# An attention and maxout kernel whose written order and list of masked tiles are replaced

## The chip, the core and the metric

The kernel runs on one core of one Trainium2 chip. The core has five engines that run side by side and wait for each other by semaphores: TensorE (PE in the profile, with PEld for its weight loads), VectorE (DVE), ScalarE (ACT), GpSimd (POOL) and SyncE (SP), which here only issues DMAs. The metric is the device time of one execution in microseconds (us), as the median of several runs.

## The reference, cut to what matters

The first part is attention over 8 batches of 8 heads, 576 tokens and 64 columns a head, in which only scores near a row's maximum count; the second is a feed-forward layer whose hidden value is the largest of three products.

```python
scores = scale * np.matmul(q, k.transpose(0, 1, 3, 2))
thresh = np.max(scores, axis=-1, keepdims=True) - tau
scores = np.where(scores >= thresh, scores, -1000000000.0)
scores = scores - np.max(scores, axis=-1, keepdims=True)
attn = np.exp(scores)
attn = attn / (np.sum(attn, axis=-1, keepdims=True) + 1e-09)
attn_out = np.matmul(attn, v)
...
x = attn_out.transpose(0, 2, 1, 3).reshape(B * S, H * D)
h = np.maximum(np.maximum(x @ w1, x @ w2), x @ w3)
out = h @ w_out
```

tau is 0.02, x is 4608 x 512, the hidden layer has 768 columns. Inputs and output are float32.

## The kernel before, in words

**Tiling.** Four heads of a batch make a quad; there are 16 quads. A quad has 9 chunks of 128 score rows in each of two halves r, so there are 144 chunks and 288 score tiles of 128 x 576. A tile's PSUM space is one of four slots of two banks; all of PE's results share these four slots. A score tile is made of two (for a quad's ninth-token chunk, index 4, four) matmuls on the two halves of PE's rows, in float32.

**One score tile.** After PE has made the scores (S), DVE takes their row maximum (m). There are two ways from there, and the string MASKED says for each tile which one is taken. In the *unmasked* way (0) DVE only reads the scores for the maximum ("unused" in the profile); ACT reads them from PSUM, subtracts the threshold and flattens what lies above (e, z<-sc,nm), and a second ACT pass over z makes the exponentials and their sum (n, z<-z). In the *masked* way (1) DVE's maximum pass also writes the negated scores to z in SBUF, so PSUM is free after it; ACT makes exponentials of z (e, z<-z,nm), and a second DVE pass compares with the threshold, multiplies and sums (k, SCALAR_TENSOR_TENSOR z<-z). Then DVE takes the reciprocals of both halves' sums (r), POOL scales both z to bfloat16 P (two p), and SP issues a transposing DMA of P (t). z has four buffers for each half r, so a chunk's z are free for the fourth chunk after it once POOL has read them. P has six buffers.

**The rest.** q and k are transposed on PE (T) and copied out by ACT (a, q) and DVE (c, k); POOL makes a copy of q with halves swapped (q) and casts v (y) and the FFN's weights (z). Once a quad's chunks are transposed, PE multiplies them by v (O), and ACT or DVE copies the result to xt (x, w). Then comes the FFN of a batch: 18 hidden pieces (6 column groups times 3 weights, tile ph) whose results ACT copies (h) and DVE joins by maximum (v), two output pieces (tile po), copied by ACT (u) and stored by SP (o), and a piece for the ninth chunk ("ninth", obr). Hidden and output pieces come in two halves on PE, F and B; B waits for the end of F, as both add to the same PSUM. The last batch's FFN is split in two parts, and its pieces aren't halved. l and g are the loads of q, k, v and of weights, issued by SP.

**What sets the order.** The string ORDER is read letter by letter at the end of the kernel, and `issue` sends each piece of work to its engine; a digit behind S, T, O or F is the PSUM slot. A small wrapper chains the instructions of each engine in that sequence, so each engine executes its own part of the text strictly in order:

```python
        def run(*a, **kw):
            ins = fn(*a, **kw)
            if self._last is not None:
                self._tc.add_manual_dep(
```

All instructions go through it, and so all have the line of its call, L91, in the profile: tiles tell them apart. Which tile comes next is fixed by the loops; only the interleaving of the kinds of work, the slot of each piece and the way of each tile (`masked`, line 311) are in the two strings. A prologue of its own (`beginning`) transposes the first quad and makes the first two score tiles.

Of the kernel before, what the change touches and what calls it, by code (L numbers as in the profile page):

```python
# [39 lines left out]
ORDER = """  # L40
lllllmlyelgS2ymylS3emgnlT0mleS1lakS2nlqermS3ylmeS0pmeS1kpS3elmS2nlzmelrmnT1pS0tcnperkT1pameS1zmteS3knpS0rnmp
emS2permeqS1mnqT3meqktepS0ncS2ntrpmS3npretprmeS1pmnS0tpmS3npmS1etpmeS0rT2mnplkeT1akgeS2qmgepmteS3rkpekntS0pe
rrnmT2pncS3ptamepS1meqtrS2meyqnS3lmqeS0pmelpknT1lpS2nmeymeS3lrkepS0tcnT2rpnmS1tpnmaprrmS0eS2pmteS1pmT3epctep
meT3O0ykntnyS2etrykpnO1wnprmaS0xptrS3meS2zmeS1mzgeS0mlnS3pmleS1pmelO2qmelpkteO0nrnklpS3nlwgxprrmS2leS0pmeF3q
tmT1eBqcF0eqkthBpnS2vS1nF3pmnF0pmBerBkepS2vhT1tnprmS0S3apmetS1zmeS2rmpeF3tmF0epBkepF1tnBvBznvS2ghS3rymnF0gmS
1eplBrkepF2tnmF3BnpvBnqvT1S0hprrcT2S3pamS1eymzF2emBeqgkF0etyS3nS1vpnmtF2pBmezBveS3prgnS0mtS1phrmT3epO2metzeF
0wpnS1gcqS2nmBqnmO3zekepgS1xvlF2nS3mtnF0rrmpBeBlpveS1lphS2mntF3zmeBrpS0evS1lpnmF2lnpS3rmleBptmS1nzvS0nS3mtpn
S2rpeF1rmepmtepS0mBepmtekF3ektekT2uBarklpukS0uqlS2urS1mlnS3pmleO0pmlepmelO2wtnkS1xrS0tepmF2myF3eBkepT1tBhcF0
nqvT2T1laByrcynS3qvS2nlqmF1tnpF0meS3pBelmBlhrrF2kpelS1vnBlprF3mnlS0pveBtprmS1hS2pmeS3tpmeS0pmF2emF1eBkeT3Bva
tF0nvqT2T3BkqlaS1nrcS3phmtS2npmF0epF1mteBqkBeqF3lnvS2lnBrvplS0hmtpS1F3meS2mteBrmepS0vnpO1rekpnO3mtnpweS2yrrt  # L50
xS1mF0yymT3epBcnS1pvS2nptF3meS0pmeBomT2hS1okeF0omF3ntBkaBervS1ponrF2vpemS0ptuS3mpeF2metknT1T3rknBparrceS0puS
3mqtuS1mpeS2mpeS3lmF0peomepS1ketqT3S2ncBqnmlqnmlO3ekluktO1urnwperrS0pxS3mptnS2mS1pempS3etmF0peF2meBlkBelS1kh
oF3nrmlF0pnBtvpBerrvS2phlS1mnpS3tmF0peS2mpeBmeF3vF1eoBkntS0vnBS2rmhpS3mepS1mteyF2mF0eyBkteBnrvT3pF1aovT2ynBp
lrcS3hplS0mnyF2lmF1elBykepBlnvT3tS0aS2vnO3rrmtpnmpeS1weptS2mS0prmO3eqtmeqF1eqlT0S2xqcBnlpmS3hlpS0meF2ymF1elB
knlF3vnBokBetS2hvS0nrrF3mpF1mpeBkBpetF2vnprS0uvnT3ptmS2aS1pmeS0trmF3epmnpkeS2tS0ermpBnmopnkS1uS2rurompS0eF3o
mpelmpeS2lkpeS0lmS1elqBmelqmetkO2unktO0erwpurkpT1txT2cS3apF0nmtT1qS2ceBqmnS1yF3hmF2eyrBpeBvptnF0pS1vnBrmtpS3
hS2pmeS0mtS1eF3meF2meBkBeF0knF1vnBBrvhpS3nvT0pF2akyF1tnBmyS0velByrmlS3phS2rlempF1lmyeF0pklBepS3tnvS2nBrmptO1
meprvepS2wnS3plmF0nF1rmepBlkeqS2lBhmtT3nyS0vnS2mqlO1emtpecT2xT0rS3pacF1eqmF2lnyBklqeT0BvlaS3khoS1qnmF0tF2pme
BrBopnvS3teprvF0pnrmS1puS2meS3prmS0epF1tmepmepT2ktBeqncT3tuS0kaS2urqmS3tnpmS1nF0pmemteS3repS1mS2lepmBelykteS
3kuO1rumplnmlpO0ewterpT2xS1cqnoS3mpF0nF2metBkeBkF1hlF3nvBlnrrS0pvlnBpmS2lhS1ymleF0mtS3epBmepF2vF1etkBnS0vnS3  # L60
rmBnpS2rhmpF0emF1pteBkpBerF3vnS2ptvnT0pBramS1pthS0mepF3meqtT2rBecpS1nvylT0ynS2pmlS3amlS1eomS0elO2rmpeomeplO3
ketnwT1F0nctF2xkBnBrvpS1hrF3pmS0qBemqS2onvF1yeF0mBopkeF3tyBnS2vqhBrlrnmpT1S0vaptS2empF1S3mpelBkeplF0vntS2rum
S1pnS0mtepF3rmepmetqS2kS0epBnmmteS1rkepS2lmuS0ulpmS1nlymT3yetF2cekeT3oBrknpamoS0npS3mnS1qtmuO0qurrmqelO2wpel
kpelS0xS3meptF2mS1peBemytF0hrkT3pBecF2nS1vpnS3rymtBpnmS0epS1vlnF3mF2etBmeBkhF0lkeF3nBrvpS1nrvBpnS2mptS0hmpeS
3meF2tmF1eBkeBlrvnT0plS3ravlpS2nlmqF0nlS1mqeBtrrmpF2eS3phBlmepS0tvepS1mS2npS3mepO0meknO1meownT3orxkT2pS0tacF
1nF2qrmeBtpS3evpBmS0tyhF1meT2yBcqoeF3rpkT2F0aptBnvBnS2pvS1hqtmF3nqT0meBrS1npvF2npmT3BactS1ervF3prmS0pueS2omp
F3ekqelmT1ntS0qcnBpmekteS2S1urrmpF0uompekS3eptS2nmS1pnmlO3ermtpekO2pnwS1ykxtyS3emS2BomeyrmepS1rukpS2uoF3meF0
opmnBtykBhpS1ervS2eptmO3pO0mxnS3txS2rmepF0empF1ekBtBevF3hkS2nS0mnBrmF1npF2vepBkBtS0hvO3emO2xkS1xerS3rpmF2mpF
0eF1kpteBnBvpF3BvtBrhkpF2S0vS1prmBptmF3eF0pveBtBhS1vS2mS3mF0F1mBkBF2vhF3keBeO0vnO1kF2kxeBwurS1rvpS0mpS2F3mpe
tmpeS0eoF1mnketBknkBurrupoF2puF0hptF3uvF2pvF1hF0tvF3rvpF2hF1vopF0vF3thF2vF1vF0hoF3vF2ovF1hF0vF3vO2uoO1wF0xF3  # L70
F2hF1vF3vF2hF1vF3vF2hF1vF3vF2hF1vF3vF2hF1vF3vF2hF1vBvF3uuooBF2uuuooo
"""


# [678 lines left out]
```

## Time and profile before

| what | value |
|---|---|
| median of 3 runs | 446.68 us (446.49 to 447.13) |
| profiled execution, span | 445.0 us |
| PE busy / weight loads | 423.6 / 313.3 us |
| DVE busy | 393.2 us |
| ACT busy | 394.4 us |
| POOL busy | 315.9 us |
| mean granted clock of TensorE | 0.992 |

The profiled execution's own time is its span, from its first instruction to its last; the runs' median lies 1.68 us above it. A group's row has the busy time of all its instructions together and the mean of one; a single instruction can begin before the one ahead of it has ended, so that the means of a packed engine add up to more than its busy time. A row "PEld sc <- ACT z: 3.5, 13, 0.4" says that weight loads for score tiles waited 3.5 us in total, 13 times, 0.4 us at most, for ACT's work on z. Matmuls are pipelined and their ends are modelled, so a busy PE says little on its pace; the start times of single pieces tell more.

### The profile page before, as it was taken

How to read it: one execution, taken by the hardware profiler on the slowest of the kernel's cores; microseconds unless marked ns; L12 is line 12 of the kernel's file. 1: busy time of each engine (PE TensorE's matmuls, PEld its weight loads, DVE VectorE, ACT ScalarE, POOL GpSimd, SP SyncE). 2: the span in 40 equal slices, each digit the busy share in tenths (PEclk: the TensorE clock that was granted, in tenths of full speed). 3: DMA queues.
4: the chain of work that ended last, by engine and by line, in shares of the span. 5: the costliest groups of instructions: out<-in, count | busy, mean ns of one | idle time of the engine just before them, and what ended most of it. 6: DMA issues, size and time to landing. Idle time of an engine off the chain costs nothing.

```text
span 445.0 us, 14089 instructions
## 1 busy us (share of the span) xinstructions
PE 423.6 (95%) x5193; PEld 313.3 (70%) x5193; DVE 393.2 (88%) x1093; ACT 394.4 (89%) x804; POOL 315.9 (71%) x422
## 2 busy tenths in 40 slices
PE   7767799999999999999999999999999999999995
PEld 5434557767787767777687867867687778777772
DVE  4989889999999999989989998999999999989641
ACT  4999999999999999999998999999999999956422
POOL 3998989989686686686768885859767789562300
PEclk9998899999999999999999999999999999999999
DMA  8989999999999978999797999899999979882902
GB/s 251 331 162 213 243 195 234 221 245 229 215 255 195 250 165 175 234 187 228 179 223 170 200 224 182 211 234 199 197 220 202 253 121 173 148 122 34 217 13 108
DMA packets 212773, 87.44 MB, mean 196 GB/s; under 512 B 185824, under 2 KB 199648, under 8 KB 212704
## 3 DMA queue, kind: packets, MB, share of 16 engines
q1 hardware_dynamic: 212000, 85.69, 93.6%
q10 hardware_dynamic: 704, 0.85, 0.6%
q8 instruction: 41, 0.67, 0.6%
q14 instruction: 28, 0.23, 0.2%
HBM read 34.60 MB, written 9.44 MB: 99 GB/s over the span
## 4 chain that ended last, share of the span: by engine, by line
PE 81%; ACT 7%; DVE 6%; issue 4%; POOL 2%; DMA 1%; DVEq 0%; POOLq 0%; ACTq 0%
PE ph L91 30%; PE sc L91 28%; PE po L91 11%; PE o L91 8%; ACT z L91 6%; PE tp L91 4%; DVE z L91 2%; DVE unused L91 2%; DMA qm<-in_q_dram 1%; POOL P L91 1%; DVE hm L91 0%; POOL w L91 0%; ACT qt L91 0%; POOL qs L91 0%; DVE hT L91 0%
## 5 line engine op out<-in xcount | busy, mean ns | idle before, releaser
L91 POOL TENSOR_SCALAR P<-z,rs 128x576 bf16<-128x576 f32 x288 | 228.1, 807 | 85.7 <-DVE rs L91 36.4
L91 PE MATMUL sc<-kt,qt 64*128 64x320 f32 (+2 forms) x640 | 179.1, 429 | 4.9 <-ACT z L91 4.4
L91 PE MATMUL sc<-kt,qs 64*128 64x256 f32 (+2 forms) x640 | 178.6, 418 | 4.7 <-ACT z L91 2.7
L91 PE MATMUL ph<-xt,w 64*128 64x288 bf16 (+2 forms) x2160 | 163.9, 283 | 0.3
L91 PEld LDWEIGHTS <-w 64*128 64x128 bf16 (+1 forms) x2160 | 124.8, 94 | 30.9 <-issue 5.3
L91 DVE TENSOR_SCALAR_CACHE_REDUCE unused<-sc 128x576 bf16<-128x576 f32 x183 | 133.2, 749 | 8.9 <-PE sc L91 8.4
L91 ACT ACTIVATE z<-sc,nm 128x576 f32<-128x576 f32 x183 | 131.3, 740 | 8.5 <-DVE unused L91 5.2
L91 ACT ACTIVATE z<-z 128x576 f32<-128x576 f32 x183 | 123.5, 680 | 0.1
L91 PEld LDWEIGHTS sc<-kt,qs 64*128 64x128 f32 (+1 forms) x640 | 92.4, 178 | 25.3 <-ACT z L91 8.1
L91 PEld LDWEIGHTS sc<-kt,qt 64*128 64x128 f32 (+1 forms) x640 | 92.4, 178 | 19.8 <-ACT z L91 9.3
L91 DVE SCALAR_TENSOR_TENSOR z<-z 128x576 f32<-128x576 f32 x105 | 84.1, 811 | 0.4 <-ACT z L91 0.4
L91 DVE TENSOR_SCALAR_CACHE_REDUCE z<-sc 128x576 f32<-128x576 f32 x105 | 77.7, 752 | 7.4 <-PE sc L91 3.4
L91 ACT ACTIVATE z<-z,nm 128x576 f32<-128x576 f32 x105 | 79.1, 773 | 3.6 <-DVE z L91 3.2
L91 POOL COPY qs<-qt 64x640 f32<-64x640 f32 (+3 forms) x68 | 47.0, 692 | 14.4 <-ACT qt L91 11.0
L91 PE MATMUL po<-wo,hT 64*128 64x512 bf16 (+1 forms) x480 | 54.0, 356 | 0.1
L91 DVE TENSOR_TENSOR hm<-ph,hm 128x576 bf16<-128x576 f32 (+2 forms) x54 | 37.0, 686 | 13.0 <-PE ph L91 11.8
L91 ACT ACTIVATE hm<-ph 128x576 bf16<-128x576 f32 (+2 forms) x54 | 32.1, 594 | 18.4 <-PE ph L91 18.1
L91 PEld LDWEIGHTS <-hT 64*128 64x128 bf16 (+1 forms) x480 | 29.6, 97 | 17.1 <-issue 2.9
L91 DVE TENSOR_TENSOR hT<-ph,hm 128x576 bf16<-128x576 f32 (+2 forms) x54 | 37.2, 688 | 3.1 <-PE ph L91 0.6
L91 PE MATMUL o<-ptq,vb 128*64 128x64 bf16 (+2 forms) x544 | 38.7, 282 | 0.0
L91 ACT ACTIVATION_READ_ACCUMULATOR z<-z 128x1 f32 x183 | 36.2, 198 | 0.0
L91 PEld LDWEIGHTS <-vb 128*64 128x64 bf16 x544 | 22.6, 111 | 15.1 <-issue 6.8
(32 smaller groups left out, 274.2 us busy)
## 6 DMA issues: line engine op xcount, KB each, us to landing
vm<-in_v_dram SPq DMA_DIRECT2D x32, 256.0 KB, 5.1
out_dram<-ob SPq DMA_DIRECT2D x31, 256.0 KB, 2.8
qm<-in_q_dram SPq DMA_DIRECT2D x15, 512.0 KB, 4.5
km<-in_k_dram SPq DMA_DIRECT2D x15, 512.0 KB, 5.4
stage<-in_moe_w_dram SPq DMA_DIRECT2D x9, 512.0 KB, 5.3
ptq<-P SPq DMA_TRANSPOSE x144, 4.1
...
```

The lines of the kernel that those rows point to most:

```text
L91: ins = fn(*a, **kw)
```

## The change

Both strings are replaced; everything else stays, the prologue, the buffers, the engine of each kind of work and every piece. The new list has 122 masked tiles in place of 105. The new text has the same letters in other places, with 122 k and 166 n in place of 105 and 183, and other slots. Below are the whole new list and the first and last four of the text's 31 lines.

```diff
--- before.py
+++ after.py
@@ -22,10 +22,10 @@
 FLAT = 2.0 ** -100
 
 MASKED = """
-010100101001000000011101001010000001100010001000101000011000100000100000
-000011111001100001001001001001000001011100101001000110001010010000010011
-000010011101100001001100100001001010001100010111000001000100000110000101
-001001001101100000110001000100100100001100100011100111010011010111110110
+110000110010010100111100010011000001110001101000101001010000100010100100
+001011101101010001001001000100010000110101001110011010001010010000011000
+110100101101110000010110100010001010001100110101001100010100001110000101
+001010011101100000100001010100100101001100101100100101110101111111110100
 """
 
 
@@ -38,37 +38,37 @@
 PBUFS = 6
 
 ORDER = """
-lllllmlyelgS2ymylS3emgnlT0mleS1lakS2nlqermS3ylmeS0pmeS1kpS3elmS2nlzmelrmnT1pS0tcnperkT1pameS1zmteS3knpS0rnmp
-emS2permeqS1mnqT3meqktepS0ncS2ntrpmS3npretprmeS1pmnS0tpmS3npmS1etpmeS0rT2mnplkeT1akgeS2qmgepmteS3rkpekntS0pe
-rrnmT2pncS3ptamepS1meqtrS2meyqnS3lmqeS0pmelpknT1lpS2nmeymeS3lrkepS0tcnT2rpnmS1tpnmaprrmS0eS2pmteS1pmT3epctep
-meT3O0ykntnyS2etrykpnO1wnprmaS0xptrS3meS2zmeS1mzgeS0mlnS3pmleS1pmelO2qmelpkteO0nrnklpS3nlwgxprrmS2leS0pmeF3q
...
-opmnBtykBhpS1ervS2eptmO3pO0mxnS3txS2rmepF0empF1ekBtBevF3hkS2nS0mnBrmF1npF2vepBkBtS0hvO3emO2xkS1xerS3rpmF2mpF
-0eF1kpteBnBvpF3BvtBrhkpF2S0vS1prmBptmF3eF0pveBtBhS1vS2mS3mF0F1mBkBF2vhF3keBeO0vnO1kF2kxeBwurS1rvpS0mpS2F3mpe
-tmpeS0eoF1mnketBknkBurrupoF2puF0hptF3uvF2pvF1hF0tvF3rvpF2hF1vopF0vF3thF2vF1vF0hoF3vF2ovF1hF0vF3vO2uoO1wF0xF3
-F2hF1vF3vF2hF1vF3vF2hF1vF3vF2hF1vF3vF2hF1vF3vF2hF1vBvF3uuooBF2uuuooo
+memkS0enmS2mS3mlellT1kaS0eemnS1mlS2ermS3rllmgS1T0S2cmS0ynqppneekqprpemeT3kS2ameS1nmreppmzenppqS3yT0mS1ceS2S0
+rmennkS1qS3krmrmppneelenpltnlmpkgpplS1zymmrS2eS0S3mlrmtlepS1T2ekemkmrkpkeaS0ttgtlptpgtS2lemrnS3ltmneT0nS1lqp
+pyelpceS0mrmnT2ppemaS1kqmS3pleqneelS0tmelttrpkrnqpmkeS2T1pcS3pS0tS1trnmnermS2pmpeemmnS0T3tzkrmnO1ptpaT2rwS3e
+ceO1emnkT2S0epxS3apS1tS2pkqpnyymmrmqpmreS3mS0S1tpmeS3ektmqeeeynkO2rlmtglpO0penwtS1xelT2lF0kzprS3mpnBlcmnS1ep
...
+kS2vynenS0pO3rmpO1S2xxmtelpS0kreF3F1BmpenmkS0BvrmehF2ppS3pBF1temypvF0BS3kvS2otnBmrmtteoO1nhO3krkxF0S2xS1ppmF
+3mBvBF2pS1BrveF0kehpS3mBF2F1pBkeprvBS0mS3vpF2hF1mBktotmvepeF0ktBF3BF2BtheevF1O0uvO3oBrkwxekvS1meS0S3pnmemrkk
+kprrF2S0F1eBBmnuuepF3huF2npvF0F3vF2hF0rpvvF3hppF2F0F3pvF2hvvF0oF3tutF2tvohF1tvF0pF3pF2hF0otvovvO1uO3xF2woF0F
+1hF3vF0F1vhvF3F0F1vF3hvF0hvF1vF3oF0vF1hF3vF0vF1F3hBuouvvF0oF1Buououo
```

More of the change, by code (lines that the diff above doesn't have):

```diff
@@ L40 @@
 ORDER = """
-lllllmlyelgS2ymylS3emgnlT0mleS1lakS2nlqermS3ylmeS0pmeS1kpS3elmS2nlzmelrmnT1pS0tcnperkT1pameS1zmteS3knpS0rnmp
-emS2permeqS1mnqT3meqktepS0ncS2ntrpmS3npretprmeS1pmnS0tpmS3npmS1etpmeS0rT2mnplkeT1akgeS2qmgepmteS3rkpekntS0pe
-rrnmT2pncS3ptamepS1meqtrS2meyqnS3lmqeS0pmelpknT1lpS2nmeymeS3lrkepS0tcnT2rpnmS1tpnmaprrmS0eS2pmteS1pmT3epctep
-meT3O0ykntnyS2etrykpnO1wnprmaS0xptrS3meS2zmeS1mzgeS0mlnS3pmleS1pmelO2qmelpkteO0nrnklpS3nlwgxprrmS2leS0pmeF3q
-tmT1eBqcF0eqkthBpnS2vS1nF3pmnF0pmBerBkepS2vhT1tnprmS0S3apmetS1zmeS2rmpeF3tmF0epBkepF1tnBvBznvS2ghS3rymnF0gmS
@@ L46 @@
[L46 to L65, printed above, removed]
@@ L66 @@
-1nF2qrmeBtpS3evpBmS0tyhF1meT2yBcqoeF3rpkT2F0aptBnvBnS2pvS1hqtmF3nqT0meBrS1npvF2npmT3BactS1ervF3prmS0pueS2omp
-F3ekqelmT1ntS0qcnBpmekteS2S1urrmpF0uompekS3eptS2nmS1pnmlO3ermtpekO2pnwS1ykxtyS3emS2BomeyrmepS1rukpS2uoF3meF0
-opmnBtykBhpS1ervS2eptmO3pO0mxnS3txS2rmepF0empF1ekBtBevF3hkS2nS0mnBrmF1npF2vepBkBtS0hvO3emO2xkS1xerS3rpmF2mpF
-0eF1kpteBnBvpF3BvtBrhkpF2S0vS1prmBptmF3eF0pveBtBhS1vS2mS3mF0F1mBkBF2vhF3keBeO0vnO1kF2kxeBwurS1rvpS0mpS2F3mpe
-tmpeS0eoF1mnketBknkBurrupoF2puF0hptF3uvF2pvF1hF0tvF3rvpF2hF1vopF0vF3thF2vF1vF0hoF3vF2ovF1hF0vF3vO2uoO1wF0xF3
@@ new lines @@
+rmF2ykpBhpqS0F1eyvpS3enmnBrmleF2BlevS0T1kS3pphS2mS0znrmymmaeF1BF2pktvetS3lpqmgtBvtgeeF0rnnS1mzeBhS2prF3ppkne
+mnqrF0eBBllvgnS1tvpzmnpF3T2pBS0rhT1etapcmrS2S3emtglemkF1S0emBF2S3vnemF0zppneBvpqS1BrnS3S2hmrT1mmO0ceewpF3S1p
+ttgelytzgpykS2mnlrllmO0kpBnlnexS1S0eqpvmF2rnmekpF3BBetzpgttS1nF0pvzmrhS2pBrmpypvneS3eS2mneF1ztlmS0BS2mS3pS0v
+S1mmrepenekrF2eplltmkmtlT3BS0aeppkumS3F1reukS2mnpemBeelkrpS0mkS3nukqpeprO2uwnmO0xqepyS1S2F0F3mmeprBT1kBecF2h
+vT0T1cBS3nvaF0mnypqnpelS1mrtqrllttBhlF2kS3mpteBvotnF0etS1mlBpprvnF2ypS3rpeBtS1S0hmpmS2eS3meF0F1ppmBmeeenkBvT
@@ new lines @@
+2avF3T0BrcT1nS2haknmS0totlpmreypF3S1BF0mpvneF2qBekpvS3BmnhtS1eF0mS2reBS3mnpeS1vmmS2qpenrepmO0wqO3ypS1enxtkrt
+pF0lmlpqT2cBoF3rnvnrS2etlpmBhpS0elmS1mplS2F3meenF0nBT2kvF1BakrpS3vS2mumpqneetoS1mtklF0enT2klrrT3acrleBS3lS1u
+mS2unypqppS0mmpmqeelS1eF3notltpkmeqpprtS2lotmetleT0tBckS1S0pmpmuyunS2rmkeeO3pwrO1kS0S3npeS2xF1mmnpF0meBBekkt
+eS3hpnF2rF1mvBBnerrhpS0S3vpS2nmmF1S0pypeBmpF2eF3tltmrBltevnkS1elnBS0vS2mpypheS3mF0meoltpyF1emlBttBeT2kvF3T0n
+vrpBaS1pcS2F0nhmnmF3eBT1BrekvqpaS2rppyprS1vnmmO0S3nenweS1meS2meS0qtmmO3rpeF1pexqppT2BkhqF0S3ckF2S1nmBBF3rmrv
@@ new lines @@
+S1BltvnlF0pS2mneehpkoBrepmT3F1vF2tkBpaetS3pS0ultlS2tvmneF1qmS3mrnS2petlnS0kpBoelpmmrpeS2nmkmruutepS3F0peS1me
+S3pBkemkrmletS2uuS1O3O0rpnmkempekrqeppwpyT2cS1T3xF0S2mBnaF3llttltotemkT1qheBF0crvnpqS2ppynBF1mreS3vmBS0S2pyp
+nmhmF3rS1BpeetF2S0mvenBkmeF1nvrF3tBkBehpF2S0nBT1vamteppF3S0kBhvmrS1S2F3mtmkeF0pyyeleBvnltllplolllS1onrmS2yBm
+ppneS3verO1mrF0newS2mBpphleF1tS3kBmS0nvmS2T3pO1qmneqpT2eckS0T3cyxF1aT2qrmBvrepqF3aS2BepmF1nS0BhF3ekrpypS2nmp
+vrBleS1S0mvnlllS2otmemnF3F1kyolpqlplemeS0unrT3BmS0eknteucpuS2tlpqS3mF1rmepkmS0leknetS2T3paBpmmlkrpS3S2mrttte
@@ new lines @@
+ulO0pueeltttmkO1eT3qppwnrcS2S0xmmrF1S3ynmBneeF2kphelF0kBBvorvF1pS3oBS2npqS0hmmreppyypF1llttS3mnrBemyvepkF0F2
+eBvpnS1BpnS3toS0mlphmmrtF1F2ekeBvBF3evS0nnT1lmBaprrtS2S1hmmpepS3F0ppT1emnqT2tlceBpaS3vS1mmS2mS0eO3mekyqwkeO1
+eenrpxF2T0F3BpS1cvrnmBnF0S2nhkBmeF3S1rBvF2S0ppqmevrBneF3hyT1mkrltottoBatppqS0S2vmF1F3BmelneS0epS2ukvnqmS3ppp
+rytmS1F0mnreS3eqmlnpttmptS2BelpmepekT1uuS2S3krmeneF0S2mcpkeS3T1prlBnaS1pmmtkeyqS3pumuS2ermnpmkeeO0eyqpO1S3wr
+kS0potxpF2nS1mmrBmkpeeF3T0BchelllnnS2vmrF1npS0mttletlBF3veS2BF1rmS0BhpkF3mevpF2BnepnpnS1BrvhmeS0rS3pmttpeS2F
@@ new lines @@
+0mmnenpF1BtBT2tloaekS3pntvvmrlS0mF2S1eoBS0rkF3temphBS2pmpprqeqepS1vS3S0pmltmymO2nkewtmkreO1pneT2xlT3pnlttF0c
+aS1BmnF2eS3BrvmpkepS0rhmeT1F3F2pqcBqBpyF1veT0BvnanS3rkhmF2eS0rmpBnnvS1mF3T0rT2cpBvtalS1F2meS0qT3upF2meecpqqS
+1olkS3tetontnmqS0mkeppemBuoS1tuS3eS0rmepS2mO1krmepO3nenxwnF1rS0pkkmprpymeepS3pmS2BemS0S2kuuF3F1pBmymetetrhBt
+kS2vynenS0pO3rmpO1S2xxmtelpS0kreF3F1BmpenmkS0BvrmehF2ppS3pBF1temypvF0BS3kvS2otnBmrmtteoO1nhO3krkxF0S2xS1ppmF
+3mBvBF2pS1BrveF0kehpS3mBF2F1pBkeprvBS0mS3vpF2hF1mBktotmvepeF0ktBF3BF2BtheevF1O0uvO3oBrkwxekvS1meS0S3pnmemrkk
```

## The prediction

> **What bounds the kernel now.** I read the page first (busy shares, then the chain), then a table of windows cut at marks of the work, then the groups and single rows that price a pass.
>
> ```profile
> span 445.0 us, 14089 instructions
> PE 423.6 (95%) x5193; PEld 313.3 (70%) x5193; DVE 393.2 (88%) x1093; ACT 394.4 (89%) x804; POOL 315.9 (71%) x422
> PE 81%; ACT 7%; DVE 6%; issue 4%; POOL 2%; DMA 1%; DVEq 0%; POOLq 0%; ACTq 0%
> ```
>
> ```profile
> core 0: us, PE busy (x) PEld busy (x) DVE busy (x) ACT busy (x) POOL busy (x), PEclk, DMA share, GB/s
> 0.00:9.00 9.00, 6.63 (x63) 5.43 (x65) 2.80 (x11) 3.37 (x8) 2.13 (x10) 1.00 0.79 220
> 9.00:68.00 59.00, 44.98 (x407) 27.40 (x409) 53.02 (x159) 57.48 (x119) 54.03 (x71) 0.94 1.06 233
> 68.00:111.00 43.00, 42.74 (x537) 31.60 (x534) 40.59 (x110) 42.21 (x90) 40.21 (x51) 1.00 1.13 236
> 111.00:355.00 244.00, 243.77 (x3175) 184.37 (x3171) 230.66 (x639) 234.51 (x474) 179.47 (x242) 1.00 1.02 208
> 355.00:410.00 55.00, 55.00 (x736) 44.12 (x734) 51.19 (x141) 44.09 (x89) 35.69 (x45) 1.00 0.71 122
> 410.00:445.00 35.00, 30.53 (x295) 20.40 (x290) 14.93 (x37) 12.76 (x29) 4.38 (x7) 0.99 0.47 114
> ```
>
> The marks: 68 is where the first hidden piece of the FFN starts, 111 the second output piece, 355 the 120th FFN piece, 410 the last score tile. Up to 68 ACT is the bound: 57.48 of 59 us, while PE has a quarter free. From 68 to 410 PE has no free time that the records show and ACT and DVE follow at 92 to 98%; the chain agrees (PE 81%). From 410 only the FFN is left and PE alone counts. The median of the runs is 446.68 us, 1.68 above the profiled span of 445.0; I add that.
>
> **The masks.** 105 ones become 122. A masked tile costs DVE its maximum (which also writes z) and a second pass, and ACT one exponential; an unmasked one costs DVE the maximum and ACT two passes. The spacing of starts in packed stretches prices this:
>
> ```profile
> 13.68 0.75 DVE L91 TENSOR_SCALAR_CACHE_REDUCE unused<-sc 128x576 bf16<-128x576 f32 x1
> 14.36 0.75 DVE L91 TENSOR_SCALAR_CACHE_REDUCE z<-sc 128x576 f32<-128x576 f32 x1
> 15.04 0.85 DVE L91 SCALAR_TENSOR_TENSOR z<-z 128x576 f32<-128x576 f32 x1
> 15.82 0.75 DVE L91 TENSOR_SCALAR_CACHE_REDUCE unused<-sc 128x576 bf16<-128x576 f32 x1
> ...
> 15.15 0.78 ACT L91 ACTIVATE z<-z,nm 128x576 f32<-128x576 f32 x1
> 15.84 0.67 ACT L91 ACTIVATE z<-z 128x576 f32<-128x576 f32 x1
> 16.61 0.74 ACT L91 ACTIVATE z<-sc,nm 128x576 f32<-128x576 f32 x1
> 17.25 0.68 ACT L91 ACTIVATE z<-z 128x576 f32<-128x576 f32 x1
> 17.91 0.67 ACT L91 ACTIVATE z<-z 128x576 f32<-128x576 f32 x1
> ```
>
> The maximum costs 0.68 either way (13.68 to 14.36 to 15.04), the second pass 0.78 (15.04 to 15.82). On ACT the masked exponential takes 0.69 (15.15 to 15.84), the unmasked pair 0.64 + 0.66. So each moved tile is +0.78 us on DVE and -0.61 on ACT; 17 are +13.3 and -10.4: DVE 393.2 + 13.3 = 406.5, ACT 394.4 - 10.4 = 384.0. DVE becomes the fuller one.
>
> Where they fall, counted in both lists by tile order: among the first 83 tiles (scores up to 111 us) 26 become 34, among the next 170 (to 355) 59 become 67, among the last 35 20 become 21.
>
> ```profile
> 7.44 0.76 DVE L91 TENSOR_SCALAR_CACHE_REDUCE unused<-sc 128x576 bf16<-128x576 f32 x1 [0.72 <-PE sc L91]
> 8.75 1.39 ACT L91 ACTIVATE z<-sc,nm 128x576 f32<-128x576 f32 x2
> ```
>
> Up to 111: ACT had 57.48 + 42.21 = 99.7 of 102 us; it loses 8 x 0.61 = 4.9. DVE had 53.02 + 40.59 = 93.6 and gains 6.2: 99.8. By these shares the two change places and nothing is won. But a lone DVE pass counts 0.75 and a packed one 0.68, so busy time overstates a fuller DVE. I also counted the operations written ahead of the second output piece, at packed spacing: DVE has 83 maxima in both, 22 second passes before and 31 after (0.74 each, between the 0.67 and 0.78 that rows show), the rest alike, in all 92.0 and 98.7 us; ACT has 55 second passes before and 47 after, one q copy and one output copy more, in all 101.0 and 96.9. ACT began tiles at 8.75, and 8.75 + 101.0 = 109.75 leaves 1.25 to the mark at 111. DVE began at 7.44: 7.44 + 98.7 + 1.25 = 107.4, a gain of 3.6. Ends: -3.6, and +1.5 if DVE's waits grow with its load. I take **-1.5**, a little to the good side of the middle, as only DVE's own waits speak for the other end.
>
> POOL reads the z that DVE has just summed, and they meet:
>
> ```profile
> 199.11 1.46 POOL L91 TENSOR_SCALAR P<-z,rs 128x576 bf16<-128x576 f32 x2
> ...
> 285.32 1.96 POOL L91 TENSOR_SCALAR P<-z,rs 128x576 bf16<-128x576 f32 x2
> ...
> 285.72 0.95 DVE L91 SCALAR_TENSOR_TENSOR z<-z 128x576 f32<-128x576 f32 x1
> L91 POOL TENSOR_SCALAR P<-z,rs 128x576 bf16<-128x576 f32 x288 | 228.1, 807 | 85.7 <-DVE rs L91 36.4 <-issue 19.8 <-ACT z L91 11.4
> ```
>
> Two normalizations take 1.46 us alone and 1.96 with a second pass of DVE beside them: +0.50. The mean of 807 ns against 730 for one alone is 288 x 0.077 = 22 us over 105 passes, 0.21 each; 17 more are +3.6 us on POOL, which idled 129 us in the span: no term, but in the first 111 us (8 passes, 1.7 us, against 102 - 94.24 = 7.8 free) it is part of the +1.5 end.
> The Trainium skill ("SBUF — State Buffer", Who interferes with whom) says that a DVE instruction with two SBUF inputs contends with a GpSimd one that reads SBUF, and whichever comes second blocks fully. The rows agree in kind; by the rule at its worst, every one of the 17 passes blocking a full 0.74, POOL would get +12.6 us instead of 3.6, still under its idle time.
>
> **The order from 111 to 410.** Both texts hold the same 2,740 letters but for the 17 second passes that change engine, and PE's pieces are interleaved alike: at the 12th, 24th, ... 288th score tile the count of FFN pieces issued differs by two at most. PE's work is therefore the same, and what can change is its waits, for PSUM banks above all:
>
> ```profile
> PEld sc L91 <- ACT z L91: 3.5, 13, 0.4
> PEld sc L91 <- DVE z L91: 2.0, 6, 0.5
> PEld tp L91 <- ACT z L91: 1.9, 6, 0.5
> DVE unused L91 <- PE sc L91: 4.7, 11, 0.9
> ACT z L91 <- DVE unused L91: 4.0, 11, 0.7
> ```
> ```profile
> 384.88 0.97 PE sc L91 x8
> 385.85 2.45 PE ph L91 x40
> ```
>
> The first three (111 to 355) are 7.4 us at stake, the price of a bank that ACT or DVE gives back late. An unmasked tile holds its bank through DVE's maximum and ACT's first pass, a masked one only through the maximum; the former fall from 183 to 166. I also counted, in PE's own order, the work between a score tile and the next piece in its bank, at 0.485 us a tile (0.97 for two, 384.88) and 0.49 a half hidden piece (2.45 for five). Unmasked tiles asked for again within 1.6 us (too early by 0.68 + 0.64 and the hand-overs): 15 of 181 before, 4 of 165 after. Masked ones within 1.3: 27 of 105, then 20 of 121. On DVE, the work between a chunk's reciprocal and the masked maximum that takes over its z four chunks later is under 1.6 us in 14 of 102 cases before, 7 of 118 after. All three say a looser order. Against it stands DVE's load: 230.66 + 8 x 0.78 = 236.9 of 244 us, 97%. Ends: -3.7 (half of 7.4) and +4 (see the first rival); I take **-1.0**. From 355 to 410 DVE gets 0.8 on 51.19 of 55: hidden, ends -0.5 and +1, taken 0.
>
> **The last pieces.** The ninth chunk's piece moves from behind the last output piece's second half to between its halves.
>
> ```profile
> 438.35 0.98 PEld L91 LDWEIGHTS <-hT 64*128 64x128 bf16 x12 [0.56 <-PE po L91]
> 439.91 1.09 ACT L91 ACTIVATE ob<-po 128x512 f32<-128x512 f32 x2 [1.74 <-issue]
> 440.64 0.42 DVE L91 COPY obr<-po 128x256 f32<-128x256 f32 x1 [4.40 <-PE po L91]
> 441.17 1.43 SPq L91 DMA_DIRECT2D out_dram<-obr  x2
> out_dram<-ob ACTq DMA_DIRECT2D x1, 256.0 KB, 2.5
> ```
>
> The second half no longer waits at its gate for the first (part of that 0.56), and the obr copy and its two stores (441.17 + 1.43, then landing) leave the end. In exchange two ob copies (1.09) and their store (2.5) follow PE's last matmul: about 440.4 + 1.1 + 2.5 = 444.0 against 445.0 less what lies behind the last landing. Taken **-0.3**, ends -0.6 and +0.5.
>
> **Stores, loads, transposes.** SP's list is reordered too: more loads now stand just ahead of a quad's last transposes (five before those of quad 5).
>
> ```profile
> 124.78 0.46 SPq L91 DMA_DIRECT2D qm<-in_q_dram  x1
> 125.34 1.28 SPq L91 DMA_TRANSPOSE ptq<-P  x1
> ptq<-P SPq DMA_TRANSPOSE x144, 4.1
> ```
>
> A load costs SP 0.46, a transpose 1.28 and 4.1 to land. From a quad's last reciprocal to its product PE has at least 4.7 us of other work before and 6.0 after, so I take 0; its loss is a rival below.
>
> Sum: -1.5 - 1.0 + 0 - 0.3 = -2.8, so 446.7 - 2.8 = 443.9 us.
>
> **Rivals.** First: DVE becomes the bound between 9 and 355. It was busy 324.3 of 346 us (53.02 + 40.59 + 230.66), 93.7%, with ACT and PE waiting for it little (the 4.0 above); 16 moved tiles make 336.8, so above 97.3% it must run or the stretch grows. At 96.2% it takes 350 us, +4: with the other terms gone, 450.7. For it: ACT as the fullest engine ran at 97.7% up to 111 but at 96.1% after. Against it: packed passes count less.
> The Trainium skill ("Perfetto Trace Analysis", Identifying the Most-Contended Engine) calls matmul occupancy a bad measure and goes by weight loads there and by occupancy elsewhere. By that rule PE (PEld 70%) isn't the bound and the fullest engine goes from ACT's 89% to DVE's 91%, so this rival would hold; the chain's 81% on PE speaks against it.
> Second: PE's waits stay as they are and the early gain is eaten by the same pacing: no change, 446.7.
> Third: transposes come late behind loads, and products wait on PE; five loads are 2.3 us, at one quad in three of sixteen, some 3 us less part of the gain: 448.5.
>
> **How the numbers follow.** Forecast 0.52, DVE as bound 0.27, no change 0.12, late transposes 0.09. Runs of this kernel differ by 0.14% (446.49 to 447.13), so 0.2%, 0.9 us, is what can be told. Low ends together are -3.6 - 3.7 - 0.5 - 0.6 = -8.4; three quarters of it, -6.2, gives 440.5. Upward the first rival with its whole 12.5 us unhidden at half is +6: 452.5. Faster 0.52, same 0.12, slower 0.36.
>
> **What would show it.** The second output piece should come by 109 us, ACT's share up to there should fall and DVE's rise above it; PE's waits for ACT's z should shrink; PE's chain share should stay near 80%. Wrong it is if DVE's groups show no idle time while PE waits for DVE's z or maximum, or if products wait for transposes.

## The result and the profile after

The changed kernel takes 460.87 us (median of 4 runs, 459.54 to 463.0) against 446.9 us for the kernel before (446.49 to 447.32) on the same chip: a ratio of 1.0315, 95% interval 1.0282 to 1.0348. It is 14 us slower; 443.9 us was forecast, and the range ended at 452.5.

The first lines of the page and the chain of the changed kernel:

```profile
span 459.3 us, 14086 instructions
PE 429.5 (94%) x5193; PEld 315.3 (69%) x5193; DVE 412.2 (90%) x1127; ACT 388.1 (85%) x770; POOL 332.8 (72%) x422
PE 62%; DVE 13%; POOL 10%; issue 7%; DMA 3%; ACT 2%; SPq 1%; POOLq 0%; DVEq 0%; ACTq 0%
```

PE's part of the chain falls from 81 to 62%. DVE, POOL, "issue" (time in which an engine waited for nothing that the profile shows) and DMA take what it lost; before, POOL and DMA had 3% together. DVE's busy time grows by 19.0 us where 13.3 were priced, POOL's by 16.9 where 3.6 were, and ACT's falls by 6.3.

Three groups of the changed kernel's page (busy us, mean ns of one, idle before them):

```profile
L91 POOL TENSOR_SCALAR P<-z,rs 128x576 bf16<-128x576 f32 x288 | 241.6, 851 | 80.0 <-DVE rs L91 45.9
L91 PE MATMUL sc<-kt,qs 64*128 64x256 f32 (+2 forms) x640 | 182.8, 421 | 9.7 <-DVE z L91 5.4
L91 DVE SCALAR_TENSOR_TENSOR z<-z 128x576 f32<-128x576 f32 x122 | 107.8, 890 | 0.7 <-ACT z L91 0.6
```

The last group in the kernel before (POOL's row of before stands in the prediction):

```profile
L91 DVE SCALAR_TENSOR_TENSOR z<-z 128x576 f32<-128x576 f32 x105 | 84.1, 811 | 0.4 <-ACT z L91 0.4
```

The number of masked tiles isn't the whole of it: one second pass has become 79 ns longer, and one normalization on POOL 44 ns (851 against 807). By a count in the traces 57 of the 122 second passes last over 0.8 us, against 24 of 105 before. The pass itself is no longer than it was: those with no work of POOL beside them take 0.75 us in the mean in both kernels. But these are 21 of 122 now, and were 38 of 105. In the first 111 us the mean was 898 ns before and is 1,049 now.

Waits of the changed kernel over the whole span (total us, times, longest):

```profile
PEld sc L91 <- ACT z L91: 12.1, 29, 1.2
PEld sc L91 <- DVE z L91: 11.5, 18, 3.5
DVE z L91 <- POOL P L91: 7.1, 10, 2.6
PE sc L91 <- DVE z L91: 5.4, 6, 3.1
POOL wo L91 <- DMA stage<-in_moe_w_out_dram: 2.8, 1, 2.8
PE o L91 <- DMA ptq<-P: 2.1, 1, 2.1
```

and of the kernel before:

```profile
PEld sc L91 <- ACT z L91: 17.3, 31, 2.2
PEld sc L91 <- DVE z L91: 4.9, 13, 0.7
DVE z L91 <- POOL P L91: 3.3, 6, 1.3
```

Read together: PE waits less for ACT's z, as forecast, and more for DVE's, which waits more for POOL to have read the old z. The last two rows of the changed kernel have no counterpart before: work that waits for a DMA.

To place the loss in time I followed PE's pieces by the written order and compared the start of each with its start before. The changed kernel is 0.6 us late at the first hidden piece, 4.2 at the 19th FFN piece (112.3), 7.9 at the second output piece (119.0 against 111.1), 8.8 at the 192nd score tile (275.7), 13.0 at the 198th (290.7), 14.2 at the last one (423.8 against 409.6). So there are two steps, 3.7 us at 112 to 119 and 4.2 at 276 to 291, and 6 us spread thin, 3.6 of them between the first hidden piece and the 19th. The two steps in the changed kernel's timeline (start, length, engine, what waited in brackets):

```profile
106.82 0.53 SPq L91 DMA_DIRECT2D stage<-in_moe_w_out_dram  x1
113.75 1.04 POOL L91 CAST wo<-stage 128x1024 bf16<-128x1024 f32 x1 [2.82 <-DMA stage<-in_moe_w_out_dram]
114.84 0.61 PE L91 MATMUL po<-wo,hT 64*128 64x512 bf16 x4 [1.50 <-POOL wo L91]
...
270.79 2.27 SPq L91 DMA_TRANSPOSE ptq<-P  x1
273.11 0.64 SPq L91 DMA_DIRECT2D vm<-in_v_dram  x1
273.85 5.42 SPq L91 DMA_TRANSPOSE ptq<-P  x3
281.34 1.19 PE L91 MATMUL o<-ptq,vb 128*64 128x512 bf16 x14 [2.08 <-DMA ptq<-P]
```

At 106.82 SP issues the last load of weights, behind four loads of q and k; the cast waits for it on POOL, and the output piece on PE for the cast. At 281 the product of quad 9 waits for transposes that SP issued between loads of v, three of them in 5.42 us. (A transpose's row holds what SP waits for the normalization, too; in the trace a normalization releases the first two of the three.)

### The profile page after: what moved, and what is told of

Same layout as the page of the kernel before. It is cut to its first block, busy times and chain, and to the rows that moved or that the text cites. A ratio compares the mean times of both kernels' runs of the same rounds, so it can differ in the third digit from the quotient of the medians.

```text
span 459.3 us, 14086 instructions
## 1 busy us (share of the span) xinstructions
PE 429.5 (94%) x5193; PEld 315.3 (69%) x5193; DVE 412.2 (90%) x1127; ACT 388.1 (85%) x770; POOL 332.8 (72%) x422
## 4 chain that ended last, share of the span: by engine, by line
PE 62%; DVE 13%; POOL 10%; issue 7%; DMA 3%; ACT 2%; SPq 1%; POOLq 0%; DVEq 0%; ACTq 0%
PE ph L91 26%; PE sc L91 21%; DVE z L91 7%; PE o L91 7%; PE po L91 7%; POOL P L91 6%; DVE unused L91 3%; PE tp L91 3%; POOL qs L91 2%; DMA ptq<-P 1%; DMA stage<-in_moe_w_dram 1%; ACT z L91 1%; SPq L91 1%; DMA qm<-in_q_dram 1%; DVE kt L91 1%
## 5 line engine op out<-in xcount | busy, mean ns | idle before, releaser
L91 POOL TENSOR_SCALAR P<-z,rs 128x576 bf16<-128x576 f32 x288 | 241.6, 851 | 80.0 <-DVE rs L91 45.9
L91 PE MATMUL sc<-kt,qs 64*128 64x256 f32 (+2 forms) x640 | 182.8, 421 | 9.7 <-DVE z L91 5.4
L91 PE MATMUL ph<-xt,w 64*128 64x288 bf16 (+2 forms) x2160 | 171.0, 283 | 0.5
L91 ACT ACTIVATE z<-sc,nm 128x576 f32<-128x576 f32 x166 | 120.5, 739 | 16.3 <-DVE unused L91 7.6
L91 DVE TENSOR_SCALAR_CACHE_REDUCE unused<-sc 128x576 bf16<-128x576 f32 x166 | 121.9, 746 | 3.4 <-PE sc L91 2.9
L91 ACT ACTIVATE z<-z 128x576 f32<-128x576 f32 x166 | 112.2, 679 | 0.6
L91 DVE SCALAR_TENSOR_TENSOR z<-z 128x576 f32<-128x576 f32 x122 | 107.8, 890 | 0.7 <-ACT z L91 0.6
L91 DVE TENSOR_SCALAR_CACHE_REDUCE z<-sc 128x576 f32<-128x576 f32 x122 | 90.7, 749 | 10.1 <-POOL P L91 7.1
L91 ACT ACTIVATE z<-z,nm 128x576 f32<-128x576 f32 x122 | 92.5, 771 | 6.7 <-DVE z L91 6.1
L91 PE MATMUL o<-ptq,vb 128*64 128x512 bf16 (+2 forms) x544 | 40.8, 286 | 2.8 <-DMA ptq<-P 2.1
```

## Experiments on the load of DVE

**The new text with as many masked tiles as before.** Sixteen of the 122 masked tiles become unmasked, each k an n at its place.

```diff
-pyelpceS0mrmnT2ppemaS1kqmS3pleqneelS0tmelttrpkrnqpmkeS2T1pcS3pS0tS1trnmnermS2pmpeemmnS0T3tzkrmnO1ptpaT2rwS3e
+pyelpceS0mrmnT2ppemaS1kqmS3pleqneelS0tmelttrpkrnqpmneS2T1pcS3pS0tS1trnmnermS2pmpeemmnS0T3tznrmnO1ptpaT2rwS3e
...
```

> The new text with 16 of its 122 masked tiles made unmasked (106; 5, 3, 7 and 1 of them by stage, k letters turned into n where they stand). Three theories. Load: the 17 extra second passes fill DVE and it becomes the bound; then most of the 14 us goes, 450 us or less. Meetings: in the new order DVE's second passes and POOL's reads of z fall on each other more often (94 of 122 passes overlap with POOL work, 57 of 105 before; mean of the pass 890 ns against 811); then the order keeps its part and 455 to 458 is left. Single waits: the jumps near 111 us (a weight cast on POOL that waits for its load) and 281 us (a product that waits for its transpose) are most of it; then 458 to 461.

It took 462.44 us, ratio to the kernel before 1.0354 (95% interval 1.0334 to 1.0375). DVE's busy time fell to 400.4 us and the time didn't. A second pass still took 883 ns in the mean: in this order the passes are long with 106 of them as with 122.

**The old text with 17 more masked tiles.** The reverse, in the old order.

```diff
-emS2permeqS1mnqT3meqktepS0ncS2ntrpmS3npretprmeS1pmnS0tpmS3npmS1etpmeS0rT2mnplkeT1akgeS2qmgepmteS3rkpekntS0pe
+emS2permeqS1mnqT3meqktepS0ncS2ntrpmS3kpretprmeS1pmnS0tpmS3npmS1etpmeS0rT2mnplkeT1akgeS2qmgepmteS3rkpekntS0pe
...
```

> The old text with 17 more masked tiles (122; 5, 3, 8 and 1 by stage, n letters turned into k where they stand). Load: 455 us or more. Meetings: 450 to 454, since the added passes were not placed for it, but the other 105 were. Single waits: the order is what matters, 446 to 449.

457.67 us, ratio 1.0245 (1.0223 to 1.0267). DVE had 407.7 us (+14.5, against my 13.3) and ACT 385.9 (-8.5, against my -10.4), so the masks themselves were priced about right. But is it their load that costs 11 us? A control tells: the same 17 tiles made masked and 17 near them unmasked, so that both engines have what they had.

```diff
-rrnmT2pncS3ptamepS1meqtrS2meyqnS3lmqeS0pmelpknT1lpS2nmeymeS3lrkepS0tcnT2rpnmS1tpnmaprrmS0eS2pmteS1pmT3epctep
+rrnmT2pkcS3ptamepS1meqtrS2meyqnS3lmqeS0pmelpknT1lpS2nmeymeS3lrnepS0tcnT2rpnmS1tpnmaprrmS0eS2pmteS1pmT3epctep
...
```

> A control for the old text with 122 masked tiles: the same 17 tiles made masked, and for each of them a near masked one made unmasked, so that 105 stay. If that run's 11 us were DVE's load, this one stays within 446 to 449. If they come from letters that stand where they were not planned, this one is slow as well, 453 to 458.

461.41 us, ratio 1.033 (1.031 to 1.035), with these lines on its page:

```profile
PE 430.9 (94%) x5193; PEld 311.3 (68%) x5193; DVE 392.8 (86%) x1093; ACT 394.6 (86%) x804; POOL 315.1 (69%) x422
PE 63%; ACT 13%; DVE 11%; issue 7%; POOL 5%; DMA 1%; DVEq 0%; POOLq 0%; ACTq 0%
```

Every engine is as busy as before (DVE 393.2, ACT 394.4, POOL 315.9) and the kernel is 15 us slower. Each engine works its list strictly in order; 34 passes that stand on another engine than the list was arranged for cost as much as the whole change, with no load added. So the 11 us of the run before it are no evidence for DVE's load; and the first run of this section, which also takes 16 passes off the engine that its text was arranged for, is none against it.

**Less work on DVE at the same places.** In the new kernel 16 second passes work on 64 of 576 columns, and the rest of those rows isn't masked; the compare of these 16 is a maximum.

```diff
+NARROW = (1, 29, 35, 0, 64, 69, 74, 85, 113, 140, 166, 172, 199, 195, 251, 261)
...
+            w = 64 if number[g, idx] * 2 + r in NARROW else S
```

> The new kernel with the second DVE pass of 16 masked tiles on 64 columns in place of 576 (left out there: the other columns' selection and sum; the same 16 tiles as were unmasked in the first run of this study), order untouched, ACT's work untouched. That is 16 x 0.65 = 10 us off DVE. Load: 452 to 455. Meetings: 16 of 122 passes no longer meet POOL, about 1 us, 459 to 460.5. Single waits: 460 to 461.

458.91 us, ratio 1.0269 (1.0233 to 1.0305): 2.0 us less for 7.1 us less work on DVE (405.1), and the two intervals overlap. By the intervals these 7.1 us are worth anything from nothing to some 4 us, so this run alone bounds DVE's load only loosely.

## Experiments on DVE's meetings with POOL

A second pass that reads z once was to take away what the passes cost each other, and leave everything else where it is; its multiplication is left out.

```diff
-            vector.scalar_tensor_tensor(out=zn, in0=zn, scalar=thr, in1=zn,
-                                        op0=OP.is_ge, op1=OP.mult, accum_out=acc)
+            vector.tensor_scalar(out=zn, in0=zn, scalar1=thr, scalar2=None,
+                                 op0=OP.is_ge, op1=OP.max, accum_out=acc)
```

In the old kernel, then in the new one:

> The old kernel with DVE's second pass as a tensor_scalar that reads z once in place of a pass that reads z as both inputs (the multiplication by z is left out, so the numerators are wrong; the number of passes and their size stay). Load and single waits: 446 to 447.5. Meetings: 443 to 446, as 57 of 105 passes overlap with POOL work, and POOL's normalizations fall from 807 ns towards 745.

> The new kernel with the same one-input second pass (the multiplication by z left out). Load: 459 to 461, as DVE has as many passes. Single waits: 458 to 461. Meetings: 448 to 454, the pass back to about 750 ns and normalizations to about 745.

The old one took 445.02 us (0.9964, 0.9948 to 0.998), the new one 453.36 (1.0148, 1.0098 to 1.0199). The new kernel's groups with that pass:

```profile
L91 POOL TENSOR_SCALAR P<-z,rs 128x576 bf16<-128x576 f32 x288 | 210.9, 744 | 110.4 <-DVE rs L91 66.5 <-issue 17.3 <-ACT z L91 6.6
L91 DVE TENSOR_SCALAR_CACHE_REDUCE z<-z 128x576 f32<-128x576 f32 x122 | 90.1, 745 | 0.7 <-ACT z L91 0.6
```

A normalization falls to 744 ns (in the old kernel too: 744), so all of its excess came from passes with two inputs. The pass now takes 745 ns in the mean, what a two-input pass takes when no work of POOL is beside it (0.75), so nothing but the meetings has gone from it. The old order loses 1.5 us to the meetings, the new one 7.5. The two steps stay: 4.5 and 4.4 us by the marks of that trace.

PE's waits for DVE shrink less than the time does. These are the rows of the changed kernel's order with the one-input pass:

```profile
PEld sc L91 <- DVE z L91: 8.9, 11, 2.7
DVE z L91 <- POOL P L91: 6.0, 4, 3.5
PE sc L91 <- DVE z L91: 5.0, 3, 2.3
```

They were 11.5, 7.1 and 5.4 us. Most of what PE waits for DVE's z in the new order is therefore there without meetings too.

The Trainium skill ("SBUF — State Buffer", Who interferes with whom) says that a DVE instruction with at most one SBUF input, outside its two-port modes, doesn't contend with GpSimd, and one with two does with GpSimd's reads. These rows agree in both halves: 744 ns with the one in the kernel, 851 in the mean with the other.

## Experiments on SP's list

**A mend by rule.** In the new kernel the four loads of q and k go behind the last load of weights, and every transpose from chunk 36 on directly behind its second normalization; then the same with the one-input pass.

```diff
-ttgelytzgpykS2mnlrllmO0kpBnlnexS1S0eqpvmF2rnmekpF3BBetzpgttS1nF0pvzmrhS2pBrmpypvneS3eS2mneF1ztlmS0BS2mS3pS0v
+ttgelytzgpykS2mnrmO0kpBnnexS1S0eqpvmF2rnmekpF3BBetzpgttllllS1nF0pvzmrhS2pBrmpypvneS3eS2mneF1ztlmS0BS2mS3pS0v
...
```

> The new kernel with SP's list alone changed: the four loads that stand ahead of the last weight load go behind it, and from the 37th chunk on each transposing DMA stands right behind its chunk's second normalization, ahead of loads and stores. Single waits: the jumps near 111 us (+3.7 us) and 281 us (+4.2 us) go, 452.5 to 454. Meetings and load: they come from DVE and POOL running late, and at most 2 us go, 459 to 461.

> The same SP list and the one-input second pass (the multiplication by z left out). If meetings and single waits are both causes and add up, 460.9 - 7.5 - 8 = 445.4, 444 to 448. If load is a third cause, 450 or more, since DVE still makes 122 second passes. If SP's list is no cause, 453 as with the old SP list.

475.11 us (1.0619, 1.0595 to 1.0643) and 464.53 (median of three runs; 1.0406, 1.0347 to 1.0464): worse. A row of the first one's waits:

```profile
PE tp L91 <- DMA qm<-in_q_dram: 13.0, 7, 6.7
```

SP too waits in order. A transpose that is written early makes SP wait for POOL, and the loads behind it come late: the load of q ahead of PE's longest wait, 6.7 us at 169, was issued at 163.9 us, and at 155.2 in the changed kernel. PE's transposes of q waited 13 us in all. The rule was mine and wrong.

**Two places only.** The loads of q and k behind the last load of weights, and the seven transposes of chunks 83 to 89 behind their normalizations.

```diff
-ttgelytzgpykS2mnlrllmO0kpBnlnexS1S0eqpvmF2rnmekpF3BBetzpgttS1nF0pvzmrhS2pBrmpypvneS3eS2mneF1ztlmS0BS2mS3pS0v
+ttgelytzgpykS2mnrmO0kpBnnexS1S0eqpvmF2rnmekpF3BBetzpgllllttS1nF0pvzmrhS2pBrmpypvneS3eS2mneF1ztlmS0BS2mS3pS0v
...
```

> The new kernel with two places of SP's list mended and everything else in its place: the last load of weights is issued ahead of the four loads of q and k that stood before it (around 105 us), and the seven transposes of the chunks 83 to 89 (quad 9, whose product came 2.6 us late around 279 us) stand directly behind their second normalization. In the new kernel's trace PE falls 3.7 us further behind the old kernel between the 19th and the 20th hidden piece and 4.2 us between the 192nd and the 198th score tile. If these two single waits make some 8 us of the loss, as the marks say: 452 to 456 us, with the 20th hidden piece at 114 to 116 us in place of 119.0 and the 198th score tile some 7 us earlier than 290.7. If the marks only show where a shortage that lies elsewhere comes due, the time that is won there is lost again behind it: 458 to 462 us.

> The same with the second pass as one that reads z once (compare, then maximum, with the same sum; the multiplication is left out), as in the run of the new kernel that took 453.36 us. If the meetings of DVE's two-input pass with POOL and the two waits are separate parts of the loss that add up: 444 to 449 us, beside 445.0 for the old kernel with the same pass, and so no more than 4 us remain for all the rest of the new order. If the waits follow from the meetings or give way to others: 451 to 454 us.

461.21 us (1.0315, 1.0282 to 1.0349): no gain, and the second case of the expectation. The second output piece came at 116.3, 2.7 us sooner, as meant. Then the product of quad 3 had this row, in the first of the two runs:

```profile
124.42 1.48 PE L91 MATMUL o<-ptq,vb 128*64 128x512 bf16 x14 [3.00 <-DMA ptq<-P]
```

SP's and POOL's rows a little earlier in that run:

```profile
110.38 5.96 SPq L91 DMA_TRANSPOSE ptq<-P  x2
116.15 2.04 POOL L91 TENSOR_SCALAR P<-z,rs 128x576 bf16<-128x576 f32 x2 [1.33 <-DMA ptq<-P]
116.39 1.83 SPq L91 DMA_DIRECT2D vm<-in_v_dram  x2
118.26 0.61 SPq L91 DMA_DIRECT2D vr<-in_v_dram  x1
118.68 1.47 POOL L91 TENSOR_SCALAR P<-z,rs 128x576 bf16<-128x576 f32 x2 [0.49 <-DMA ptq<-P]
118.97 3.39 SPq L91 DMA_TRANSPOSE ptq<-P  x2
```

The second and third of three transposes behind the four loads take 5.96 us to issue, three loads of v follow, and the quad's last two transposes stand behind those. The rows show a second way, by the six buffers of P: POOL's normalizations wait 1.33 and 0.49 us for transposes to free one, and end at 120.15, after SP has reached the next transpose (118.97). By these rows it is the slow transposes rather than the loads of v that hold the last two up. What was won at one late transfer was given to the next. With the one-input pass the same text took 449.94 us (1.0065, 1.0044 to 1.0085), 3.4 less than without the mend, between the two cases of its expectation.

**The next places.** I followed the hand-over: quad 3's last three transposes ahead of the loads of v, quad 9's last two and all of quad 10's behind their normalizations.

```diff
-S1mmrepenekrF2eplltmkmtlT3BS0aeppkumS3F1reukS2mnpemBeelkrpS0mkS3nukqpeprO2uwnmO0xqepyS1S2F0F3mmeprBT1kBecF2h
+lS0vS1mmrepenekrF2epmkmlT3BS0aeppkumS3F1reukS2mnpemBeelkrpS0mkS3nukqpeprO2uwnmO0xqepyS1S2F0F3mmeprBT1kBecF2h
...
```

> The new kernel as in the run with the two waits mended (461.21 us), with the places where its loss came back mended too: the last three transposes of quad 3, whose product came 3.8 us late there, stand directly behind their second normalizations and ahead of three loads of v; the last two of quad 9 and all of quad 10 (1.4 and 0.9 us late) likewise, with the loads and stores that stood between them behind. Nothing on PE, DVE, ACT or POOL is moved. If the products' transposes are a part of the loss by themselves: 453 to 457 us, with no product over 1 us late. If what is won on SP is lost again to DVE's and POOL's meetings, which the single waits had covered: 458 to 462 us with no product late.

> The same with the second pass as one that reads z once (the multiplication is left out). The run before it with that pass took 449.94 us, with 10.2 us of products waiting for their transposes in quads 1, 3, 9 and 10. If the new order's loss is made of the meetings and of SP's places and of nothing else, 444 to 447 us, the time of the old kernel with that pass (445.0 us). If something third is in it, 448 to 451 us although the products of quads 3, 9 and 10 come in time.

461.66 us (1.0315, 1.0284 to 1.0346) and 451.15 (1.0085, 1.0054 to 1.0116). The first time fits the second case, but with a product late, and the second lies just above its own second case. At the 210th score tile the first stood 9.2 us behind the kernel before, 4.4 better than the changed kernel, and the second 1.1 ahead; then quad 10's product came 4.4 and 4.6 us late, since SP issued that quad's transposes, stores and loads in turn without a pause.

**Stores and loads behind that quad's transposes.** The lines are against the run before.

```diff
-reulO0ptueelmkO1eT3qpptwnrcS2S0xmmrF1S3ynmBneeF2kphelF0kBBvorvF1ptS3oBS2npqS0hmmreptpyyptF1llS3mnrBemyvepkF0
+uO0ptueemkO1eT3qpptllwnrcS2S0xmmrF1S3ynmBneeF2kpheF0kBBvrvF1ptS3BS2npqS0hmmreptpyyptF1S3mnrBemyvepkF0F2eBvpt
...
```

> The new kernel as in the run with the transposes of quads 3, 9 and 10 mended (461.66 us), where quad 10's product came 4.4 us late all the same, since SP worked without a pause from 277 to 302 us on transposes, loads and stores in turn: five stores' and six loads' places between these transposes are moved behind the last of them. Up to the 210th score tile that run stood 9.2 us behind the old kernel, 4.4 less than the new one, and lost 5.1 us in the next six tiles. If quad 10's product then comes in time and nothing else is displaced: 455 to 458 us. If the load on SP in this stretch is lost at a later place: 459 to 462 us.

> The same with the second pass as one that reads z once (the multiplication is left out). The run before it with that pass stood 1.1 us ahead of the old kernel at the 210th score tile, as the old kernel with that pass does (1.5 us ahead), and lost 4.2 us to quad 10's product. If meetings and SP's places are all of the loss: 444 to 447 us. If something third comes behind 300 us: 448 to 450 us.

455.46 us (1.0206, 1.0187 to 1.0224), as the first case had it, and 447.3 us with the one-input pass (1.001, 0.9985 to 1.0035; 444.56 to 449.35), at the edge of its first case. Page and chain of the first, in which no product waits longer than 1.1 us:

```profile
PE 427.4 (94%) x5193; PEld 312.7 (69%) x5193; DVE 411.1 (91%) x1127; ACT 387.8 (85%) x770; POOL 332.5 (73%) x422
PE 60%; POOL 13%; DVE 10%; issue 8%; DMA 5%; ACT 3%; SPq 0%; POOLq 0%; DVEq 0%; ACTq 0%
```

and of the second:

```profile
PE 422.8 (95%) x5193; PEld 312.8 (70%) x5193; DVE 396.4 (89%) x1127; ACT 384.3 (86%) x770; POOL 290.4 (65%) x422
PE 75%; DVE 8%; DMA 6%; POOL 5%; issue 4%; ACT 1%; SPq 0%; POOLq 0%; DVEq 0%
```

With SP's list mended, DVE and POOL are as busy as in the changed kernel and the time is 5.4 us less. With the two-input pass gone too it is another 8.2 less, and PE has 75% of the chain again. The two steps together are 13.6 us (460.9 to 447.3), and the new order with both stands 2.3 us above the old one with the same pass (445.0); in that run's trace the products of quads 1 and 11 still come 3.5 and 1.6 us late. This speaks on the 17 more passes by themselves, too: DVE is 8.6 us busier there than in the old order with that pass (396.4 against 387.8), and they and all else that is new cost 2.3 us.

The two parts don't quite add up. The one-input pass is worth 7.5 us with the changed kernel's list of SP and 8.2 with the last one, but 10.6, 11.3 and 10.5 with the three other lists. With two inputs the first mends won nothing, and with one 3.4 us.

**The new tail alone, in the old text.**

```diff
-F2hF1vF3vF2hF1vF3vF2hF1vF3vF2hF1vF3vF2hF1vF3vF2hF1vF3vF2hF1vBvF3uuooBF2uuuooo
+F2hF1vF3vF2hF1vF3vF2hF1vF3vF2hF1vF3vF2hF1vF3vF2hF1vF3vF2hF1vBvF3uuooF2Buououo
```

> The old kernel with the new text's end alone: the ninth chunk's output piece stands between the two halves of the last output piece, and each of the last stores behind its copy. The prediction gave this part 0.3 us less. In the new kernel the time from PE's last work to the end of the span was 4.6 us, against 4.4 us in the old one, so a reading of that trace gives it nothing: 446.5 to 447.2 us. If the prediction's term holds, 446.3 to 446.7 us; if the ninth piece's copy delays the last output piece's, 447.2 to 448.5 us.

446.62 us against 446.59: 1.0001 (0.9989 to 1.0012). It is worth nothing that can be measured; the interval, 0.5 us to either side, is too wide to tell 0.3 us. None of the runs that do all of the work beats the kernel before.

## Why the prediction was wrong

**POOL's meetings with DVE: the step that failed.** I worked out 0.21 us a pass from the old order, had "17 more are +3.6 us on POOL, which idled 129 us in the span: no term", and gave DVE's side of the meeting no price at all. Both halves fail. The price of a pass isn't a constant of the kernel, it is set by what stands beside it: POOL's normalizations grew by 13.5 us (228.1 to 241.6), and DVE's passes by 79 ns each, 9.6 us over 122. Against 744 ns for a normalization without such passes that is 0.17 us a pass on POOL before (my 0.21 took 730 ns for one alone) and 0.25 after. And POOL's idle time was no cover: the runs put the meetings at 7.5 to 8.2 us in the new order (10.5 to 11.3 with SP's three other lists) and 1.5 in the old one, 6 to 7 us of the loss. By which waits they reach PE isn't shown. A late normalization holds the z that DVE's next masked maximum needs (7.1 us of waits in place of 3.3), and that maximum holds the PSUM bank for PE (11.5 and 5.4 in place of 4.9 and 0.6); but with the one-input pass these waits are still 6.0, 8.9 and 5.0. An example, two engines of the changed kernel:

```profile
103.83 1.03 POOL L91 CAST wo<-stage 128x1024 bf16<-128x1024 f32 x1
103.88 1.60 DVE L91 SCALAR_TENSOR_TENSOR z<-z 128x576 f32<-128x576 f32 x1
104.84 1.97 POOL L91 TENSOR_SCALAR P<-z,rs 128x576 bf16<-128x576 f32 x2
```

The pass ends 0.6 us after POOL's cast has ended (104.86), 1.60 us in place of 0.75, and the two normalizations behind the cast take 1.97 us in place of 1.46. So both engines pay, and the first to be in the way isn't even a normalization; I had counted those alone. My price of 0.78 for the second pass hid a meeting as well: POOL had work beside the row at 15.04, and passes without it start 0.68 us apart in packed stretches of the same trace.

**Stores, loads, transposes: "so I take 0".** This was the second failed step, 5.4 us by the mended list. I compared PE's cover with a transpose's 1.28 us and 4.1 to land, and didn't add up what stands ahead of a quad's last transposes in SP's list. By my own rows two normalizations (1.46) and 4.1 to land are 5.6 of the 6.0 us of cover, which leaves no room for even one load of 0.46. And 1.28 is near the low end: in the kernel before a transpose kept SP 1.36 us in the middle of the 144, 2.0 or more in a quarter of them and 4.8 at most, waits for the normalization included. The third rival was right in kind, and wrong in place and size: the product that waited was quad 9's, not quad 5's, and the first loss at 111 us was a load of weights for POOL.

**The masks: +13.3 on DVE, -10.4 on ACT.** About right: 14.5 and -8.5 in the old text. The rest of the 19.0 came with the order.

**Start, -1.5.** The shares came as predicted: up to 111 us DVE has 57.19 + 41.24 = 98.4 us (forecast 99.8) and ACT 53.97 + 40.14 = 94.1 (94.8), from these rows of the changed kernel's windows (columns as in the prediction):

```profile
9.00:68.00 59.00, 44.59 (x400) 28.06 (x401) 57.19 (x161) 53.97 (x107) 55.73 (x68) 0.91 1.02 225
68.00:111.00 43.00, 40.73 (x496) 29.75 (x495) 41.24 (x109) 40.14 (x83) 39.64 (x49) 1.00 1.07 228
111.00:355.00 244.00, 237.68 (x3021) 178.06 (x3020) 228.33 (x629) 221.68 (x440) 181.38 (x231) 0.99 1.02 197
```

The time didn't follow: the second output piece came at 119.0, not by 109. PE's busy time falls from 42.74 to 40.73 in the second stretch and from 243.77 to 237.68 in the third, which is room for waits.

**Order, -1.0.** I counted, within PE's list and within DVE's, how much stands between a bank or a z and its next use, and found it looser. The same three waits between 111 and 355 us, in the changed kernel:

```profile
PEld sc L91 <- ACT z L91: 4.4, 14, 0.5
PEld tp L91 <- ACT z L91: 1.9, 3, 1.4
PEld sc L91 <- DVE z L91: 1.8, 5, 0.7
```

They make 8.1 us against 7.4: nothing was won. A count within one engine's list can't see when the work that it waits for runs on another engine. From 355 on, 0 was right: the last score tile is 14.2 us late, as the 252nd was.

**Last pieces, -0.3.** From PE's end to the end of the span it is 4.7 us after and 4.4 before, and the run with that part alone shows no gain, within 0.5 us.

**The rival that DVE becomes the bound.** It ended on the right side with the wrong cause. DVE is at 97% in the first window and 94% in the third; narrower passes on it won 2.0 us of the 14 for 7.1 us less work, 17 more passes and all else that is new cost 2.3 us where the meetings were gone and SP's list mended, and the control with equal loads lost 15. (The upper end of the range, from this rival, was mis-added too: 446.7 + 6 is 452.7, not 452.5.) The rule of the fullest engine (the Trainium skill, "Perfetto Trace Analysis", Identifying the Most-Contended Engine) would name DVE, 90%; here taking work from DVE at the same places won little.

What stays open: why the new order brings more passes beside POOL's work, whether the longer passes on DVE or the longer ones on POOL cost the 7 us (the one-input pass shortens both, and DVE's busy time falls by 15.5 us with it) and by which waits, why the pass's worth varies with SP's list, and the last 2 us. And in the old text, where the passes stayed at 801 ns, 34 swapped passes cost 15 us by waits that I didn't separate.
